# A fixed instruction order from a search, paced loads and 64x64 turns at the start of an attention and FFN kernel

## The chip, the cores and the metric

The kernel runs on one core of a Trainium2 chip. The metric is the device time of one execution in microseconds. A profile shows one execution: its span is the time from the first to the last instruction, and its engines are PE (TensorE's matmuls), PEld (TensorE's weight loads), DVE (VectorE), ACT (ScalarE), POOL (GpSimd) and SP (SyncE, which only issues DMAs).

## What is computed

Attention with squared relu instead of softmax, and a gated FFN on the result:

```python
# q, k, v: (8, 12, 448, 64) float32
scores = q @ k.T / sqrt(64)
attn = maximum(scores, 0) ** 2 / 448
x = (attn @ v)              # -> 3584 tokens x 768
out = (maximum(x @ w_gate, 0) * (x @ w_val)) @ w_out     # 768 -> 1536 -> 768, float32
```

## The kernel before

**Tiling.** Four heads of one batch row make a quad; there are 8 x 3 quads. A quad's keys lie on partitions 64 to 127 and its queries on 0 to 63, in seven slots of 64 positions (`NT`). For its scores the quad has to be turned, so that the head dimension lies on the partitions: for batch row 0 by `transpose_first` (L540 and L547 hold the transposes), for row 1 by `transpose_pe` (L588), for the rest by a DMA transpose on SP (`transpose_dma`, L618, after a permuting copy L610 or L612). L513 and L515 copy the turned quad out of PSUM. A score step (`Attention.s`, L686) multiplies 64x64 tiles, four array positions at a time; relu (L697 on ScalarE, L699 on VectorE) and square (L709, L711) follow, then the product with the values (`pv`, L728) and its copy to `xT` (L744, L746). Row 0 is done in two parts, 192 and 256 positions of its queries, so that the FFN can begin early.

**FFN.** `gv_plain` (L793) is the gate and value product of rows 0 and 1, in blocks of 128 columns of the weights. Later rows go in pairs by a Strassen scheme (`gv_strassen`, L902; `out_both`, L1017), with evictions of partial products to float32 tiles `f` (L849, L851 on ScalarE; L853, L855 on VectorE) and sums by VectorE (L1007). Outputs leave by `store` (L989): two DMAs on SP per tile, for the last ones one on SP and one on ScalarE.

**Loads.** GpSimd's DMAs (`dma_in`, L404) cast float32 to bf16 on the way; keys, queries and values come per quad, the weights in column blocks (`load_gv`) and quarters (`load_out`). At most eight are out at a time. For quad 0, the queries' first three slots come as float32 by two hardware DMAs (L455, on ScalarE's and SP's queues, 96 KB each) and are cast by VectorE (L457); its keys are the first two DMAs of GpSimd.

**Order.** `plan` is a list scheduler that runs when the program is built. It has a time for each operation, gives an operation to the engine that ends it first, takes PSUM banks and buffers as they come free, and fills TensorE's modelled gaps in the first 32 us with matmuls on a constant tile (`filler`, L1171), which compute nothing. Three strings (`PE_ORDER`, `LOAD_ORDER`, `AHEAD`) set the order on TensorE, that of the loads, and priorities. The instructions are issued in the order of the planned starts; each engine works its own off in that order.

Of the kernel before, what the change touches and what calls it, by code (L numbers as in the profile page):

```python
# [15 lines left out]
class Res:  # L16


    def __init__(self, n):
        self.free = {i: 0.0 for i in range(n)}  # L20
        self.by = {}

    def at(self, i):

        t, op = self.free[i], self.by.get(i)
        return t if op is None else max(t, op.end + Planner.LATE[1])


class Buf:


    def __init__(self, res, among=None, width=1):
        self.res, self.width = res, width
        self.among = among if among is not None else sorted(res.free)
        self.readers, self.last, self.idx = 0, 0.0, None

    def pick(self, now=0.0):

        best = None
        for i in self.among:  # L40
            if all(i + w in self.res.free for w in range(self.width)):
                t = max(self.res.at(i + w) for w in range(self.width))
                if best is None or max(t, now) < max(best[0], now):
                    best = (t, i)
        return best


class Op:


    def __init__(self, engs, emit, deps=(), alloc=(), reads=(), mode=None, grp=None):
        self.engs, self.emit = engs, emit
        self.deps, self.alloc, self.reads = list(deps), list(alloc), list(reads)
        self.mode, self.grp = mode, grp
# [4 lines left out]
        self.start = self.end = self.eng = None  # L59
        for b in self.reads:  # L60
            b.readers += 1


class Planner:
    NOUT = 8
    SWITCH = 0.1
    BIAS = 0.2
    MARGIN = 1.5
    LATE = (2.0, 1.0, 0.3)
    TO_LOAD, LOADED = 2.35, 0.95  # L70
    TO_TURN, TURNED, TURN = 1.7, 0.8, 3.65
    ISSUE = 0.28
    TO_HW = 1.9
    COLD = 4.6, 1.6
    FILL_FROM = 0.4
    FILL_COLD = 5.5
    FILL_UNTIL = 32.0
    FILL_MARGIN = 0.1
    GV_ORDER = '1256734'
    OUT_ORDER = 'ab1cd572364'  # L80
    END_ORDER = ('517364', '523')
    BUFFERS = (3, 11, 3, 4, 4, 4, 3)
    PV_PAIRS = (0, 0)
    JOIN = True
    TWO_QUEUES = True
    SPLIT = False
    MERGE = False
    URGENT = {'sh': -0.5, 'perm': 0.5}
    YIELD = {'sq': 0.1, 'sh': 0.1}
    PV_AT_0 = 0  # L90
    QT = 3
    PART = 6
    PV_AT = (1, 1)
    T_AT = (1, 1)
    MORE_UNTIL = 6
    BY_PE = 6
    ORDER = 'LV610ab2c3x4oy5rzqp'

    def __init__(self, banks):
        self.banks = banks  # L100
        self.t = {"POOL": 1.25, "DVE": 0.85, "ACT": 0.74, "SP": 0.74}
        self.ops = []
        self.mode = None
        self.dma_t = 0.0
        self.queues = [], []
        self.loads = []

    def free_at(self, bank):
        return self.banks.free.get(bank, 1e9)

    def now(self, op):
        return self.t.get("PE", 0.0) if "PE" in op.engs else 0.0

    def ready(self, op):
        r = 0.0
        for d in op.deps:
            if d.end is None:
                return None
            if d.eng != "PE" or "PE" not in op.engs:
                r = max(r, d.end + (self.LATE[0] if d.xbar else self.LATE[2] if d.load else 0.0))  # L120
        for b in op.alloc:
            p = b.pick(self.now(op))
            if p is None:
                return None
            r = max(r, p[0])
        return r

    def best(self, op):
        r = self.ready(op)
        if r is None:  # L130
            return None
        c = None
        for e, (occ, busy) in op.engs.items():
            if e in ("DVE", "ACT"):
                r = max([r] + [d.end + self.MARGIN for d in op.deps if d.load and not d.hw])
            s = max(r, self.t.get(e, 0.0))
            if e == "PE" and op.mode != self.mode:
                s = max(r, self.t.get(e, 0.0) + self.SWITCH)
            f = s + busy + (self.BIAS if e == "DVE" and len(op.engs) > 1 else 0.0)
            if c is None or f < c[0]:  # L140
                c = (f, s, e)
        return c[1], c[2], r

    def rates(self, a, b):

        if not (a and b):
            return 1.0, 1.0
        share = a[0][0].share
        return 1.0 - share, share

    def flow(self, a, b, t, until):
        while t < until and (a or b):
            rates = self.rates(a, b)
            d = min([q[0][1] / r for q, r in zip((a, b), rates) if q] + [until - t])
            t += d
            for q, r, post in zip((a, b), rates, (self.LOADED, self.TURNED)):
                if q:
                    q[0][1] -= d * r
                    if q[0][1] < 1e-6:
                        q.pop(0)[0].end = t + post  # L160
# [1124 lines left out]
```

## Time and profile before

| | us |
|---|---|
| device time, median of 3 runs (401.0 to 403.32) | 402.75 |
| span of the profiled execution | 402.3 |
| TensorE busy | 393.8 |
| VectorE busy | 326.1 |
| ScalarE busy | 274.0 |
| GpSimd busy | 75.7 |
| fillers L1171 on TensorE | 34 matmuls |
| first FFN matmul (L793) starts at | 27.5 |

The profiled execution's span is 0.4 us under the median of the runs. The page gives busy time by engine; its second part cuts the span into 40 slices and writes the busy share of each in tenths, with the granted TensorE clock below. The chain of waits follows the last instruction back to what released it, step by step, and so shows which engine set the end at each moment. Windows give the busy time of every engine in chosen stretches.

### The profile page before, as it was taken

The numbers are of one execution on the slowest core, as the hardware profiler recorded it, in microseconds if no ns is written. First come the engines' busy times: TensorE is split into PE (matmuls) and PEld (weight loads), VectorE is DVE, ScalarE is ACT, GpSimd is POOL, SyncE is SP. The second block draws the span as 40 slices with busy tenths as digits, with TensorE's granted clock in tenths as the row PEclk, the third lists the DMA queues.
The fourth block names the chain that finished last, engine by engine and source line by source line (L and its number), as shares of the span: only waits on it lengthen the run. The fifth ranks groups of instructions, "written<-read, shape, count | busy, mean of one in ns | idle before, by whom it ended". The sixth has DMA issues, their size and how long they took to land.

```text
span 402.3 us, 8737 instructions
## 1 busy us (share of the span) xinstructions
PE 393.8 (98%) x3472; PEld 210.1 (52%) x3472; DVE 326.1 (81%) x568; ACT 274.0 (68%) x399; POOL 75.7 (19%) x121
## 2 busy tenths in 40 slices
PE   6999999999999999999999999999999999999995
PEld 3567745454455554444455554444555555555563
DVE  5688788999989879969988989888789967758662
ACT  3697786477979728969879868878788843333221
POOL 7946441020430110311030221300100000000000
PEclk9799999999999999999999999999999999999999
DMA  8999999948988995193698796682224320000245
GB/s 121 192 198 199 201 193 183 147 48 136 124 144 171 162 116 115 26 145 56 84 141 153 152 131 129 82 92 47 46 37 99 80 59 2 0 0 2 59 118 139
DMA packets 77337, 43.54 MB, mean 108 GB/s; under 512 B 40688, under 2 KB 77296, under 8 KB 77296
## 3 DMA queue, kind: packets, MB, share of 16 engines
q0 software_dynamic: 34640, 23.50, 43.1%
q1 hardware_dynamic: 42192, 18.98, 26.5%
q8 instruction: 27, 0.44, 0.5%
q10 hardware_dynamic: 464, 0.49, 0.4%
q14 instruction: 14, 0.11, 0.1%
HBM read 47.19 MB, written 11.01 MB: 145 GB/s over the span
## 4 chain that ended last, share of the span: by engine, by line
PE 95%; DMA 1%; DVE 1%; POOL 0%; issue 0%; ACT 0%; POOLq 0%
PE ps L902 36%; PE ps L1017 25%; PE ps L793 14%; PE ps L686 10%; PE ps L728 8%; DMA gvT<-in_q_dram 1%; PE ps L1171 1%; PE ps L540 1%; PE ps L588 1%; DVE at L711 1%; POOL gvT L404 0%; DVE at L699 0%; DVE qkT L515 0%; DVE f L853 0%; ACT xT L744 0%
## 5 line engine op out<-in xcount | busy, mean ns | idle before, releaser
L697 ACT ACTIVATE at<-ps 128x896 bf16<-128x896 f32 (+4 forms) x116 | 103.2, 906 | 22.6 <-PE ps L686 21.8
L849 ACT COPY f<-ps 128x448 f32<-128x448 f32 x99 | 52.1, 532 | 45.8 <-PE ps L902 34.2
L709 ACT ACTIVATE at<-at 128x896 bf16<-128x896 bf16 (+1 forms) x72 | 67.0, 947 | 2.0 <-DVE at L699 1.2
L711 DVE TENSOR_TENSOR at<-at 128x896 bf16<-128x896 bf16 (+4 forms) x99 | 58.9, 607 | 9.2 <-ACT at L697 8.1
L699 DVE TENSOR_SCALAR at<-ps 128x896 bf16<-128x896 f32 (+4 forms) x55 | 58.4, 1064 | 6.9 <-PE ps L686 6.2
L404 POOL DMA_DIRECT2D vv<-in_v_dram x44 | 26.7, 611 | 165.5 <-PE ps L686 152.5
L686 PE MATMUL ps<-qkT 64*64 64x448 bf16 (+2 forms) x756 | 51.5, 342 | 1.0 <-ACT xT L744 0.3
L902 PE MATMUL ps<-xT,gvT 128*128 128x448 bf16 x216 | 50.9, 353 | 0.0
L902 PE MATMUL ps<-sx,wv 128*128 128x448 bf16 x216 | 50.6, 353 | 0.1
L902 PE MATMUL ps<-xT,wg 128*128 128x448 bf16 x216 | 49.7, 353 | 0.0
L902 PEld LDWEIGHTS <-gvT 128*128 128x128 bf16 x324 | 30.7, 98 | 30.5 <-issue 3.2
L1017 PEld LDWEIGHTS <-sh 128*128 128x128 bf16 x312 | 29.5, 98 | 22.9 <-issue 3.6
L1017 PEld LDWEIGHTS <-hT 128*128 128x128 bf16 x270 | 25.3, 98 | 20.5 <-issue 4.5
L1017 PE MATMUL ps<-wo,hT 128*128 128x384 bf16 x192 | 35.6, 327 | 0.0
L686 PEld LDWEIGHTS <-qkT 64*64 64x64 bf16 x756 | 19.5, 106 | 27.5 <-issue 22.4
L728 PE MATMUL ps<-at,vv 64*64 64x448 bf16 (+2 forms) x700 | 33.4, 327 | 0.0
L1007 DVE SCALAR_TENSOR_TENSOR o<-ps,f 128x384 f32<-128x384 f32 x41 | 22.5, 554 | 12.1 <-PE ps L1017 7.2
L902 PEld LDWEIGHTS <-wv 128*128 128x128 bf16 x216 | 20.6, 98 | 21.0 <-issue 2.8
L793 PE MATMUL ps<-xT,wv 128*128 128x448 bf16 (+2 forms) x180 | 31.3, 316 | 0.0
L902 PEld LDWEIGHTS <-wg 128*128 128x128 bf16 x216 | 20.6, 98 | 19.9 <-issue 1.7
L851 ACT ACTIVATE f<-ps 128x384 f32<-128x384 f32 x37 | 18.2, 491 | 18.6 <-PE ps L1017 18.3
L793 PE MATMUL ps<-xT,wg 128*128 128x448 bf16 (+2 forms) x180 | 30.6, 315 | 0.0
(72 smaller groups left out, 495.5 us busy)
## 6 DMA issues: line engine op xcount, KB each, us to landing
out_dram<-o SPq DMA_DIRECT2D x108, 96.0 KB, 2.2
vv<-in_v_dram POOLq DMA_DIRECT2D x44, 112.0 KB, 5.1
raw<-in_k_dram POOLq DMA_DIRECT2D x18, 224.0 KB, 5.4
raw<-in_q_dram POOLq DMA_DIRECT2D x18, 224.0 KB, 6.0
wo<-in_moe_w_out_dram POOLq DMA_DIRECT2D x4, 576.0 KB, 16.7
wg<-in_moe_w_gate_dram POOLq DMA_DIRECT2D x5, 384.0 KB, 9.9
wv<-in_moe_w_val_dram POOLq DMA_DIRECT2D x5, 384.0 KB, 10.6
gvT<-in_k_dram POOLq DMA_DIRECT2D x5, 224.0 KB, 6.3
```

What stands on the lines that cost most here:

```text
L404: op = Op({"POOL": (0.5 + 0.0004 * n_desc,) * 2}, lambda: nc.gpsimd.dma_start(out=dst(), in_=src), deps=deps, alloc=alloc)
L686: nc.tensor.matmul(banks()[64 * j:64 * j + 64, z, h2], lhsT=self.k_of(j, h2, k), rhs=self.q_of(j, h2), start=True, stop=True)
L697: nc.scalar.activation(self.at_of(i, m), banks(), AF.Relu)
L699: nc.vector.tensor_scalar_max(self.at_of(i, m), banks(), 0.0)
L709: nc.scalar.activation(a, a, AF.Square)
L711: nc.vector.tensor_tensor(a, a, a, ALU.mult)
L728: nc.tensor.matmul(ps[64 * h2:64 * h2 + 64, ps2.idx + j, :n], lhsT=st.v_of(j, h2, c), rhs=self.at_of(c)[64 * j:64 * j + 64, 0, h2], start= ...
L793: nc.tensor.matmul(ps[:, pb.idx, z * n:(z + 1) * n], lhsT=w[:, kd, fc], rhs=xT_t[xbuf[b].idx][:, kd, cols], start=(kd == 0), stop=(kd == K ...
L849: nc.scalar.copy(dst, src)
L902: nc.tensor.matmul(ps[:, pb.idx, :S], lhsT=w(g)[:, fc], rhs=rhs, start=start and g == 0, stop=stop and g == KH - 1, skip_group_check=True)
L1007: op = Op({"DVE": V384}, lambda: nc.vector.scalar_tensor_tensor(o_t[ob.idx], ps[:, pb.idx, :OH], float(out_scale), f_t[fb.idx][:, :OH], AL ...
L1017: nc.tensor.matmul(ps[:, pb.idx, :OH], lhsT=lhs(kf), rhs=rhs(kf), start=start and kf == 0, stop=kf == FH - 1, skip_group_check=True)
```

## The change

1. The scheduler is gone. `PLAN`, a string of some 5,300 characters, holds the order of all operations and fillers, the engine of each and every buffer and bank; `replay` reads it. The classes keep only what `replay` needs, and options that had one value are written out.
2. `hold_back` runs ahead of each of the first 46 loads of GpSimd. It goes back over the issued loads until their modelled times sum to 4.5 us, and has GpSimd copy one element of the load before these; that copy waits until the load has landed.
3. Quad 0's keys (all) and queries (three slots) come as float32 by the hardware queues of ScalarE and SP, 448 and 192 KB, and are cast in two and one operations. They are kept slot by slot with the heads side by side, so that one transpose turns two heads (`paired`).
4. Turns by TensorE are made of 64x64 transposes; keys and queries go to separate PSUM banks and are copied out whole.
5. A store may be issued from SP or from ScalarE; the plan says which.

The order that results: TensorE has 6946 instructions before and 7126 after. Fillers go from 34 to 24. The transposes on TensorE are 36 of 128x64, 48+48 of 64x64 and 84 of 128x64 before; 20 with 64 rows by 128 columns and 296 of 64x64 after. Changes of the array's shape go from 155 to 138 in all, and from 133 to 130 counted from the first L793 on. All other matmuls are the same in number and shape. GpSimd has 30 of the one-element copies. VectorE has 568 instructions before and 596 after; ScalarE issues 22 stores instead of 4, and 33 evictions (21 of 448 and 12 of 384 columns) go from ScalarE to VectorE.

```diff
-PE_ORDER = (...)
-LOAD_ORDER = (...)
-AHEAD = (...)
+IN_FLIGHT, HELD = 4.5, 46
+PLAN = (...)
+def replay(ops, filler):
+    text = iter(PLAN)
...
+    while True:
...
+        if i == FILL:
+            filler(number(), number(), number(2))
+            continue
+        left.remove(i)
+        op = ops[i]
+        op.eng = list(op.engs)[number() if len(op.engs) > 1 else 0]
+        for b in op.alloc:
+            b.idx = number()
+        op.emit()

+    seen = pool.tile([1, 1], BF16, name="seen")
+    issued, waited = [], [-1]
+    def hold_back():
+        k, held = len(issued), 0.0
+        if k >= HELD:
+            return
+        while k > 0 and held < IN_FLIGHT:
+            k -= 1
+            held += issued[k][1]
+        k -= 1
+        if held >= IN_FLIGHT and k > waited[0]:
+            d = issued[k][0]
+            at = d[tuple(slice(0, 1) for _ in d.shape)].rearrange(FLAT[len(d.shape)])
+            nc.gpsimd.tensor_copy(seen[0:1, 0:1], at)
+            waited[0] = k

     def dma_in(dst, src, n_desc, us, deps=(), alloc=(), share=0.25):
-        op = Op({"POOL": (0.5 + 0.0004 * n_desc,) * 2}, lambda: nc.gpsimd.dma_start(out=dst(), in_=src),
-                deps=deps, alloc=alloc)
+        def emit():
+            d = dst()
+            hold_back()
+            issued.append((d, op.load))
+            nc.gpsimd.dma_start(out=d, in_=src)

     def first_loads(st, src):
-            k_op = dma_in(lambda: st.raw()[64:128, hs], src(k)[:, hs], 128, 0.05)
-            ld = Op({eng: (0.65, 0.65)}, lambda: queue.dma_start(out=wide[0:64, hs], in_=src(q, 0, QT)[:, hs]))
-            cv = Op({"DVE": (0.46, 0.55)}, lambda: nc.vector.tensor_copy(st.raw()[0:64, hs, :QT], wide[0:64, hs]), deps=[ld])
+        kl = fetch(k, slice(64, 128), NT, "ACT", nc.scalar, 3.6)
+        ql = fetch(q, slice(0, 64), QT, "SP", nc.sync, 3.4)
+        st.k_ops = [narrow(kl, slice(64, 128), slice(2 * j, 2 * j + 2), NT, True) for j in range(2)]
+        st.q_ops = [narrow(ql, slice(0, 64), slice(0, 4), QT, True)]

+    def turn(bank_of, st, a, slots, js=(0, 1), shift=0):
+        rows = slice(64 * a, 64 * a + 64)
+        for t in slots:
+            for j in js:
+                pb, c = bank_of(a, j)
+                cols = slice(c + (t - shift) * P2, c + (t - shift + 1) * P2)
+                if st.paired and not shift:
+                    nc.tensor.transpose(ps_b[:, pb.idx, cols], st.paired(rows)[:, t, 2 * j:2 * j + 2].rearrange("p h d -> p (h d)"),
+                                        ident[rows, rows])
+                    continue
+                for h2 in range(2):
+                    x = st.late()[:, 2 * j + h2, t - shift] if st.paired else st.raw()[rows, 2 * j + h2, t, :]
+                    nc.tensor.transpose(ps_b[64 * h2:64 * h2 + 64, pb.idx, cols], x, ident[rows, rows])

     def transpose_pe(b, g):
-                        nc.tensor.transpose(ps_b[64 * h2:64 * h2 + 64, ps2.idx + j, t * 128:(t + 1) * 128],
-                                            st.raw()[:, 2 * j + h2, t, :], ident)
-        op = pe(emit, 0.93, deps=st.qk_ops + [id_op], alloc=[ps2, st.qt_buf], mode="128x64")
+            for t in range(NT):
+                for a in range(2):
+                    turn(lambda a, j: (pbs[a], j * S), st, a, (t,))
+        op = pe(emit, 0.47, deps=st.qk_ops + [id_op], alloc=[*pbs, st.qt_buf], mode="64x64")

     def store(ob, op, where):
-        for eng, queue, zs in (("SP", nc.sync, (0,)), ("ACT", nc.scalar, (1,))) if last else (("SP", nc.sync, (0, 1)),):
+        for engs, zs in ((("SP",), (0,)), (("ACT",), (1,))) if last else ((("SP", "ACT"), (0, 1)),):
```

More of the change, by code (lines that the diff above doesn't have):

```diff
@@ L372 @@
     f_t = [pool.tile([128, S], FP32, name=f"f{i}") for i in range(N_F)]
[L373 removed]
+    g_t = [pool.tile([128, S], BF16, name=f"g{i}") for i in range(N_G)]
     o_t = [pool.tile([128, OH], FP32, name=f"o{i}") for i in range(N_O)]
@@ new lines, in narrow @@
+        def narrow(ld, rows, hs, slots, act):
+            n = (hs.stop - hs.start) * slots * D
+            cv = Op({"DVE": (0.08 + n / 1850.0, 0.15 + n / 1850.0)}, None, deps=[ld])
+            if act:
+                cv.engs["ACT"] = vec(n)["ACT"]
+            cv.emit = lambda: copy_out(cv.eng, paired(rows)[:, :slots, hs], wide[rows, hs, :slots].rearrange("p h t d -> p t h d"))
+            cv.kind = "wide"
+            others.append(cv)
+            return cv
+        kl = fetch(k, slice(64, 128), NT, "ACT", nc.scalar, 3.6)
@@ L1160, with filler @@
     others.extend([still_op, id_op])
[L1162 to L1175 removed]
+    def filler(bank, n, width):
+        for _ in range(n):
+            nc.tensor.matmul(ps[:, bank, :width], lhsT=still[:, :128], rhs=still[:, :width], start=True, stop=True)
     for g in range(NQ):
@@ L1251 @@
         out_both(2 * p, p + 2, To_ops)
-    for op in plan(first, att, ffn, others, pool_ops, still_op, filler, r_ps):
-        op.emit()
+    replay([*sum(first, []), *att, *[o for o, _ in ffn], *others, *pool_ops], filler)
 _INS = ['q', 'k', 'v', 'moe_w_gate', 'moe_w_val', 'moe_w_out']
```

596 lines of the change are left out of this document (209 added, 387 removed).

## The prediction

> **What bounds the kernel now.** I read the page from the top: busy shares and slices first, then windows over the start, the chain of waits, and TensorE's timeline.
>
> ```profile
> PE 393.8 (98%) x3472; PEld 210.1 (52%) x3472; DVE 326.1 (81%) x568; ACT 274.0 (68%) x399; POOL 75.7 (19%) x121
> ...
> PE   6999999999999999999999999999999999999995
> ...
> PEclk9799999999999999999999999999999999999999
> ```
>
> TensorE is busy nearly everywhere; only the first slices and the last are thinner, and only the second has a lower granted clock. "Busy" includes L1171, matmuls on a constant tile that fill modelled gaps and compute nothing. So I ask how much of the start is real work. These windows are cut where the granted clock changes (5.47, 8.88, 15.70) and where the first real FFN matmul starts, L793 at 27.5 us in the timeline; columns are busy us and instructions of each engine, clock, DMA share, GB/s.
>
> ```profile
> 5.47:8.87 3.40, 1.96 (x45) 1.02 (x43) 1.67 (x4) 1.44 (x3) 2.19 (x5) 1.00 1.22 167
> 8.88:15.70 6.82, 6.64 (x87) 3.60 (x87) 3.53 (x8) 3.50 (x5) 5.95 (x9) 0.50 1.38 192
> 15.71:27.50 11.79, 10.58 (x288) 7.32 (x287) 10.15 (x19) 10.43 (x16) 7.83 (x11) 1.00 1.50 194
> ```
>
> From 5.47 to 15.70 VectorE and ScalarE work 10.1 of 20.4 engine-us (1.67+3.53+1.44+3.50): 50%. From 15.71 to 27.50 it is 20.6 of 23.6: 87%. They relu, square and copy the scores that the FFN needs, and in the first stretch they lack scores. The start is bound by the arrival of the first three quads, then by these two engines. Afterwards the chain is TensorE's own:
>
> ```profile
> 9.06 1.53 PE ps L540 x19
> ...
> 39.19 0.91 PE ps L588 x28
> 40.10 0.50 PE ps L686 x8
> ...
> 68.03 0.38 PE ps L686 x8
> 68.41 11.46 PE ps L793 x60
> ...
> 326.01 44.28 PE ps L902 x234
> ...
> 372.81 25.36 PE ps L1017 x156
> ```
>
> 44.28/234 = 0.189 us per 448 columns and 25.36/156 = 0.163 per 384: no room there. Eight score matmuls take 0.38 us behind others of their shape, 0.50 when the array shape has just changed; 60 FFN matmuls take 11.46 instead of 60 x 0.189 = 11.34. **A change of array shape costs about 0.12 us.** TensorE ends at 398.2; the last add, its two stores and the closing waits take the other 4.1 us.
>
> **The change, part by part.** The sum is against this execution's span, 402.3 us, 0.4 under the median 402.75 of the runs; I add the difference to the median.
>
> *FFN and later, from the first L793 on.* The matmuls are the same ones. (a) Three quads are turned by 56 transposes of 64x64 each instead of 28 of 128x64 (L588, 0.91 a quad). The 64x64 form exists in L547, two positions at a time:
>
> ```profile
> 16.96 0.69 PE L547 MATMUL ps<-ident,gvT 64*64 64x64 bf16 x32 [0.41 <-DVE at L699]
> ...
> 24.46 0.44 PE L547 MATMUL ps<-ident,gvT 64*64 64x64 bf16 x16
> ```
>
> Sixteen more cost 0.25 us, 15.6 ns each. The new form goes over both halves of the rows and both of the columns, four positions: between 7.8 ns each (0.44 a quad) and 15.6 (0.87). I take 0.50: the scores of L686 use four positions, and eight of them cost two columns' streams (0.38 = 2 x 0.189). 3 x (0.91-0.50) = 1.2 us; bounds 0.1 to 1.4. (b) In the two orders I count changes of shape from the first FFN matmul on: 133 before, 130 after; 3 x 0.12 = 0.4. (c) Twelve more 256-column score matmuls stand ahead of that point: 3 x 0.109 = 0.3. The new order also moves 33 evictions from ScalarE to VectorE (0.62 and 0.55 us each, groups L853 and L855) and 18 store issues from SP to ScalarE (0.5 us each in the trace); fewer relus and narrow copies on VectorE give some back. VectorE goes from 326 to about 342 us, 87% of a 393 us stretch; nothing on it becomes the bound, but its cover is thinner. Sum: 1.9 us.
>
> *The start.* The new TensorE order holds 24 filler matmuls in place of 34. Quad 0's keys and queries come as fp32 by the hardware queues, 640 KB issued at 0.74 us, and are narrowed on VectorE and ScalarE; GpSimd begins with quads 1 and 2. Before, two hardware loads of 96 KB took 3.3 and 3.5 us to land. I estimate 4.0 to 5.0 for the larger ones, so 4.8 to 5.7. Two casts of 896 elements (0.35 us for 384, so about 0.6 each), the turns and the copies put the first scores at 6.9 (6.3 to 8.0), against 6.85: no gain there. The gain is behind it. On GpSimd's queue, 752 KB lie up to the last query that quads 1 and 2 need, 864 before; before, that byte count landed at 10.0 and 10.6 us. All their turns stand together ahead of their scores, so these flow from about 10.3; before, quad 1's began at 10.4 and quad 2's at 13.0, at half clock. Early relus of quad 0 cover 9 to 10.3. I let both engines be dense from 9.0.
>
> Their work up to the first FFN matmul: 30.7 engine-us from 5.47 on (10.1+20.6), plus 2.0 for wider casts and 0.9 for more, smaller copies: 33.6. About 5 are done by 9.0 (casts 2.0, first copies 1.3, first relus and squares). 28.6 at 87% (the third window) need 16.4 us, at 93% (VectorE 4.78 and ScalarE 4.52 in 25 to 30 us) 15.4. The first FFN matmul comes at **24.9** (23.9 to 26): 2.6 us earlier.
>
> The clock belongs to it. It was 1.00 for 3.4 us with TensorE busy 1.96 of them, then 0.50 for 6.8. The new order has ten fillers and the turns just there, so I expect it to stay at 1.00. [...]
>
> *Loads.* Weights come behind. In the old order the tightest weight landed 3.7 us before its use (34.2, used 37.9). Reading the new GpSimd order by bytes against the old issues and landings of the trace, with the FFN at 24.9: one key load at 31.0 against a turn at 30.4; weights at 36.0, 37.9 and 42.1 against 36.4, 38.1 and 42.0. The slack is gone: 0.5 us lost. *Holding back* adds 30 one-element copies on GpSimd, each waiting for a landing, with the next DMA issue behind it. No copy of GpSimd is in the trace: between a 0.035 us step (its four memsets) and a whole square of VectorE, 0.61 (L711). I take 0.2: 30 x 0.2 = 6 us, beside 30 us of issues in the first 46 us, hidden while the queue keeps the 4.5 us of transfers that the code's constant allows. At the upper end it is the second rival.
>
> Sum: 2.6+1.9-0.5 = 4.0 faster: 398.3 in span, **398.7 us**; own range 396.5 to 400.5.
>
> **Rivals.** *Loads become the bound* (0.17). For it: slack 0 to 0.7 us at four places between 30 and 45 us. Against: the DMA is full anyway (about 195 GB/s until 60 us). Loads 5% slower are 1.8 us late at 42: 400.5.
>
> *GpSimd starves the loads, slower than before* (0.10). Each copy reads SBUF while VectorE runs squares back to back. If each waits a whole one, 30 x 0.61 = 18.3 on top of 30 us of issues make 48 in 46 us: the queue runs dry between issues, and loads are 4 to 6 us late by 45 us with nothing to cover it. With 6.5 lost: 405. It decides from about 0.5 us a copy. [...]
>
> *The start gains little* (0.15): hardware loads land late (the change not doing what it says), or the clock drops again and eight fillers take 2.8 us instead of 1.4. FFN from 26.7: 400.5.
>
> *The fixed order stalls* (0.08): engine, bank and order are written out, and the old chain shows one such wait of TensorE (0.64 us on an eviction of VectorE's, L853 at 239.4). Four more of 0.6 us each: 401.
>
> **Chances.** Forecast 0.50. About 0.5% (2 us) is what a measurement of this kernel tells from no change, so faster is below 400.7 and slower above 404.8. Forecast 0.50, plus 0.10, 0.08 and 0.02 of the first, third and fourth rival: faster 0.70; same 0.19; slower 0.11 (second rival 0.10, strays 0.01). The range leaves out the second rival and some 0.08 at the ends: 396.5 to 402.5.
>
> **What would show it.** Right: first FFN matmul near 25 us; granted clock 1.00 from about 5.5 us on; VectorE and ScalarE over 85% busy from 10 us; turns of 0.5 us; waits of TensorE for DMA under 1 us in 28 to 45; TensorE's end near 394. Wrong: a clock of 0.50 past 9 us, turns near 0.9, waits for wg or wv, GpSimd copies over 0.5 us, or an FFN start beyond 26.5.

## The result and the profile after

The changed kernel takes **419.07 us** (median of 4 runs, 417.86 to 419.98) beside 403.03 for the kernel before (4 runs, 401.0 to 404.13): ratio 1.0408, 95% interval 1.0363 to 1.0454. It is 16 us slower; the forecast was 398.7, and its range ended at 402.5. The profiled execution has a span of 417.0 us. Medians here and below are of all runs of a kernel; ratios leave out a single slow run, over 1.5% above the fastest of its kernel, which six of the kernels below have.

The page after, its busy shares, its slices and the granted clock:

```profile
PE 395.5 (95%) x3562; PEld 209.0 (50%) x3562; DVE 333.4 (80%) x596; ACT 259.6 (62%) x374; POOL 81.3 (19%) x149
...
PE   7798989989997999999999899999999999999996
...
PEclk9999999999997999999999899999999999999999
```

A slice is 10.4 us. TensorE's now have dips at 31 to 42, 52 to 63, 83 to 94, 125 to 136 and 229 to 240 us, and the granted clock is below full in two slices, the 13th (125 to 136 us) and the 23rd (229 to 240). To place the loss I line the two traces up by work: at which time has each done the same share of the useful matmuls? The changed kernel is 2.1 us ahead at 24 us, just before its first FFN matmul (26.1), level at 36, 0.8 to 1.3 ahead at 42 to 55, 1.4 behind at 72, 3.3 at 91, 4.6 at 124, **10.4 at 141, 15.3 at 253**, and keeps that to the end. So the last 160 us are alike, and the loss is made in a slow slope up to 124 us and in two steps.

TensorE's waits in the changed kernel, longest in total first (us in total, times, longest):

```profile
PE ps L901 <- DVE o L891: 5.4, 2, 3.0
PE ps L569 <- DVE xT L628: 1.7, 1, 1.7
...
PE ps L610 <- DMA gvT<-in_v_dram: 1.4, 1, 1.4
...
PE ps L569 <- issue: 1.1, 1, 1.1
...
PE ps L675 <- DMA wg<-in_moe_w_gate_dram: 0.7, 1, 0.7
```

The two waits of the first line are the two steps. Four timelines of the changed kernel around the first (start, length, engine, line, operation; in brackets the idle time before it and what ended it): TensorE, VectorE, SP's queue, GpSimd's queue.

```profile
130.83 2.08 PE L901 MATMUL ps<-wo,hT 128*128 128x384 bf16 x6 [3.00 <-DVE o L891]
```
```profile
124.78 0.55 DVE L891 SCALAR_TENSOR_TENSOR o<-ps,f 128x384 f32<-128x384 f32 x1
125.25 0.62 DVE L509 COPY perm<-raw 128x1792 bf16<-128x1792 bf16 x1
130.22 0.56 DVE L891 SCALAR_TENSOR_TENSOR o<-ps,f 128x384 f32<-128x384 f32 x1 [4.35 <-DMA out_dram<-o]
```
```profile
118.43 2.90 SPq L515 DMA_TRANSPOSE qkT<-perm  x2
121.39 3.72 SPq L871 DMA_DIRECT2D out_dram<-o  x4
125.93 4.56 SPq L515 DMA_TRANSPOSE qkT<-perm  x2
```
```profile
122.32 1.20 POOL L263 DMA_DIRECT2D vv<-in_v_dram  x2 [8.49 <-PE ps L610]
123.49 0.65 POOL L263 DMA_DIRECT2D raw<-in_k_dram  x1
124.10 0.64 POOL L263 DMA_DIRECT2D vv<-in_v_dram  x1
124.69 0.68 POOL L263 DMA_DIRECT2D raw<-in_q_dram  x1
126.16 0.61 POOL L263 DMA_DIRECT2D raw<-in_k_dram  x1 [0.79 <-DVE perm L509]
```

An output tile is written at 116.5 us; its store stands on SP behind two DMA transposes and leaves at 121.4. Then GpSimd sends six loads within 5 us. The store issued at 123.67 lands at 130.09, 6.4 us later; the constant in the code (`st.land`) is 2.5. VectorE needs that tile, waits 4.35 us with everything behind it, and TensorE, whose PSUM bank it should empty, waits 3.0. VectorE's waits for output tiles, summed over the trace:

```profile
DVE o L891 <- DMA out_dram<-o: 8.0, 3, 4.4
```

What that does to the clock shows in windows (busy us, instructions, of PE, PEld, DVE, ACT, POOL; clock; DMA; GB/s):

```profile
126.36:129.76 3.40, 1.47 (x14) 0.60 (x7) 0.00 (x0) 1.75 (x2) 0.41 (x1) 1.00 1.15 179
129.77:136.60 6.83, 5.77 (x24) 2.24 (x24) 5.95 (x11) 2.46 (x4) 0.00 (x0) 0.50 1.32 158
...
228.76:232.16 3.40, 1.02 (x10) 0.63 (x7) 1.47 (x4) 3.37 (x5) 0.00 (x0) 1.00 1.47 220
232.17:235.58 3.41, 3.41 (x13) 1.57 (x12) 2.33 (x5) 0.51 (x2) 0.00 (x0) 0.50 0.69 159
```

Each wait brings TensorE to half clock, for 6.83 and 3.41 us; the first drop begins 1.1 us before its wait has ended. Wait and half clock together are the steps of 5.8 and 4.7 us, taken between the same points of the work in both traces. 6.83 is twice 3.41, and the windows of 3.40 us ahead of the two drops have TensorE busy 1.47 and 1.02 us.

The traces say more on it. In each of the 20 profiled executions the drops begin on a grid of 3.41 us (in the changed kernel at 129.77, 232.17 and 416.49 us, 30 and 54 steps apart; in the kernel before at 8.88 and 401.41, 115 steps; the last one of each lies behind TensorE's end), and the grid lies elsewhere in each execution. Cut along it, all 14 windows at full clock with TensorE busy under 0.45 of the window were followed by half clock. Between 0.45 and 0.6 some were and some were not: 1.96 of 3.40 us (0.58) was, at the start of the kernel before, while the window of 88.81 to 92.22 us of the changed kernel, busy 0.51, was not, and a wait of 3.1 us in the run with the copies in the old order (below) fell on two windows, busy 0.59 and 0.51, and was not. So what a wait costs depends on where it falls on the grid as well as on its length.

In the kernel before, stores issued between 120 and 140 us land as slowly (median 5.5 us, longest 7.8), yet in the profiled execution VectorE never waits for a tile: its order has slack there. In a second look at that kernel (below) VectorE waits once, 1.6 us at 123.9, and TensorE not at all.

### The profile page after: what moved, and what is told of

Same layout as the page of the kernel before. It is cut to its first block, busy times and chain, and to the rows that moved or that the text cites. A ratio compares the mean times of both kernels' runs of the same rounds, so it can differ in the third digit from the quotient of the medians.

```text
span 417.0 us, 8952 instructions
## 1 busy us (share of the span) xinstructions
PE 395.5 (95%) x3562; PEld 209.0 (50%) x3562; DVE 333.4 (80%) x596; ACT 259.6 (62%) x374; POOL 81.3 (19%) x149
## 4 chain that ended last, share of the span: by engine, by line
PE 73%; DMA 19%; POOL 3%; issue 2%; SPq 1%; DVE 1%; ACT 0%; POOLq 0%; DVEq 0%
PE ps L784 35%; PE ps L901 23%; PE ps L569 6%; DMA wg<-in_moe_w_gate_dram 6%; PE ps L610 5%; PE ps L675 4%; DMA wo<-in_moe_w_out_dram 4%; DMA wv<-in_moe_w_val_dram 3%; DMA out_dram<-o 3%; DMA gvT<-in_k_dram 3%; POOL seen L252 1%; SPq L871 1%; POOL gvT L263 1%; POOL raw L263 0%; DVE o L891 0%
## 5 line engine op out<-in xcount | busy, mean ns | idle before, releaser
L579 ACT ACTIVATE at<-ps 128x896 bf16<-128x896 f32 (+4 forms) x121 | 105.8, 902 | 37.2 <-PE ps L569 36.5
L731 ACT COPY f<-ps 128x448 f32<-128x448 f32 x78 | 41.0, 537 | 54.3 <-PE ps L784 26.0
L591 ACT ACTIVATE at<-at 128x896 bf16<-128x896 bf16 (+2 forms) x73 | 67.3, 949 | 4.1 <-DVE at L581 3.6
L581 DVE TENSOR_SCALAR at<-ps 128x896 bf16<-128x896 f32 (+2 forms) x50 | 54.0, 1089 | 18.0 <-PE ps L569 17.5
L593 DVE TENSOR_TENSOR at<-at 128x896 bf16<-128x896 bf16 (+4 forms) x98 | 57.2, 607 | 4.1 <-ACT at L579 3.8
L569 PE MATMUL ps<-qkT 64*64 64x448 bf16 (+2 forms) x756 | 52.9, 342 | 5.0 <-DVE xT L628 1.7
L675 PE MATMUL ps<-xT,wg 128*128 128x448 bf16 (+2 forms) x180 | 31.2, 315 | 1.1 <-DMA wg<-in_moe_w_gate_dram 0.7
L263 POOL DMA_DIRECT2D raw<-in_k_dram x18 | 11.4, 631 | 104.4 <-DVE perm L509 93.1
L901 PE MATMUL ps<-wo,sh 128*128 128x384 bf16 x156 | 31.5, 342 | 0.0
## 6 DMA issues: line engine op xcount, KB each, us to landing
wo<-in_moe_w_out_dram POOLq DMA_DIRECT2D x4, 576.0 KB, 10.1
```

The costliest lines, as they stand in the source:

```text
L263: nc.gpsimd.dma_start(out=d, in_=src)
L569: nc.tensor.matmul(banks()[64 * j:64 * j + 64, z, h2], lhsT=self.k_of(j, h2, k), rhs=self.q_of(j, h2), start=True, stop=True)
L579: nc.scalar.activation(self.at_of(i, m), banks(), AF.Relu)
L581: nc.vector.tensor_scalar_max(self.at_of(i, m), banks(), 0.0)
L591: nc.scalar.activation(a, a, AF.Square)
L593: nc.vector.tensor_tensor(a, a, a, ALU.mult)
```

## The experiments

Theory A: the written-out order needs output tiles back too soon for stores that share the DMA with loads. B: holding back starves the early loads. C: the one-element copies themselves cost. D, formed on the way: TensorE's instructions arrive late.

### Stores beside loads (A)

**Late loads left out.** `dma_in` issues nothing for q, k, v of rows 4 to 7.

```diff
-            nc.gpsimd.dma_start(out=d, in_=src)
+            if not left_out:                       # left_out = b >= 4
+                nc.gpsimd.dma_start(out=d, in_=src)
```

> The changed kernel without GpSimd's loads of q, k and v for batch rows 4 to 7 (issued from 106 us on); these rows are computed from what lies in the buffers. Theory A with the loads as the cause of the slow stores (five to seven loads are issued within 4 us just ahead of the stores, and both kinds of packets alternate on the same DMA engines): the stores land in 2.5 to 3 us, the waits of TensorE for o at 131 and 231 us and the half clocks behind them go: 407 to 410. If the DMA transposes on SP's queue are the cause instead: both waits stay, 416 to 419. Theory B: all of its loss lies earlier, 416 to 419 too unless the waits go.

Measured: 409.49 us, ratio to before 1.0173 (1.0112 to 1.0234). Stores of 120 to 140 us land in 2.23 us (median; 4.08 in the changed kernel). Of the two waits this is left:

```profile
PE ps L903 <- DVE o L893: 1.1, 2, 0.7
```

That is within 407 to 410: the loads are the main cause of the slow stores. In the changed kernel, from 123.7 to 130.1 us, 1147 packets of GpSimd's queue and SP's begin, and from one to the next the queue changes 373 times.

**Transposes left out.** `for a in range(2 if b < 4 else 0)` around the DMA transpose.

> The changed kernel without the DMA transposes of batch rows 4 to 7 on SP's queue (the copies ahead of them stay; scores of these rows use what lies in the buffers). Theory A with the loads as the cause: the stores still land 5 us or more after their issue in both places, at least one of the two waits of TensorE stays, 411 to 418. Theory A with the transposes as the cause (stores queue behind them on SP, and share the DMA): both waits go, 407 to 410.

Measured: 414.32 us, 1.0291 (1.0221 to 1.0361). Both waits stay (4.5 us in total, longest 2.4), the first step shrinks by 2.9 us. That is within 411 to 418, for the loads as the cause; the transposes have a part in it, the smaller one.

**Stores on ScalarE's queue.** `if op.land and len(op.engs) > 1: op.eng = "ACT"` in `replay`.

> The changed kernel with all stores but the last ones issued by ScalarE; SP keeps the DMA transposes. At the first place the store of a tile written at 116.5 us is issued at 121.4 us, behind two DMA transposes on SP, and then meets the loads. Theory A with SP's queue as half of the cause: that store leaves at 117, the wait of TensorE at 131 us goes or falls under 1 us; the second place (stores ahead of the transposes, behind the loads) stays: 411 to 415. If only the loads count: both waits stay, 417 to 420. ScalarE is 62% busy and has 0.5 us more per store issue; if that costs, 420 to 424.

Measured: 427.28 us, 1.0565 (1.0491 to 1.064), worse than all that was expected. ScalarE now waits itself for an output tile (4.45 us at 135.5), TensorE 3.7 us for it, and more of the same comes at 404 and 413 us.

```profile
ACT o L735 <- DMA out_dram<-o: 12.0, 3, 5.3
...
PE ps L571 <- ACT o L735: 3.7, 1, 3.7
```

A free queue is no remedy where the engine behind it has other work.

**Late loads paced.** Here nothing is left out: `hold_back` goes on after the 46th load with 1.2 in place of 4.5 us of transfers in flight; in the second kernel it goes on only from the 56th load.

```diff
-        if k >= HELD:
+        if HELD <= k < FROM:                       # first kernel: FROM = HELD = 46; second: FROM = 55
             return
-        while k > 0 and held < IN_FLIGHT:
+        most = IN_FLIGHT if k < HELD else LATER    # LATER = 1.2
+        while k > 0 and held < most:
```

> The changed kernel with the holding back carried on for the loads after the 46th, at 1.2 us of modelled transfers (about one load of a quad at a time). Theory A with the loads as the cause: fewer packets of loads stand beside the stores, which land in 3 to 4 us, the waits for o shrink to under 1.5 us each, 409 to 414, if the loads themselves don't come too late. If they do (each load then waits for the one before it, some 2.5 us apiece, 10 us per quad against about 14 us between quads): new waits of TensorE for q, k, v, 418 to 425. Rival: no change, 418 to 420.

Measured: 420.98 us, 1.0385 (1.0293 to 1.0476). Both effects are there: the steps shrink by 5.0 and 2.2 us, but w_out, now held too, lands late, VectorE waits 9.8 us for it and TensorE 8.5:

```profile
DVE woT L720 <- DMA wo<-in_moe_w_out_dram: 9.8, 1, 9.8
...
PE ps L568 <- DVE xT L627: 8.5, 1, 8.5
```

> The changed kernel with the holding back carried on at 1.2 us of modelled transfers from the 56th load on (from 85 us; the loads of w_out and of rows 2 and 3 ahead of it go out as they are). Carried on from the 47th load, it cut the two waits for o tiles by 5.0 and 2.1 us but made w_out 9 us late. Theory A with the loads as the cause: the gain stays and that loss goes, 411 to 414. Rival (the two effects hang together): 418 to 421.

Measured: **408.78 us**, 1.014 (1.008 to 1.0199): 10 us better than the changed kernel, with the same work. GpSimd's queue at the first place (line numbers are higher by one):

```profile
123.83 0.18 POOL L253 COPY seen<-vv 1x1 bf16<-1x1 bf16 x1 [2.84 <-DMA vv<-in_v_dram]
124.28 0.62 POOL L264 DMA_DIRECT2D raw<-in_k_dram  x1 [0.28 <-issue]
124.89 0.18 POOL L253 COPY seen<-vv 1x1 bf16<-1x1 bf16 x1
125.02 0.60 POOL L264 DMA_DIRECT2D vv<-in_v_dram  x1
125.66 0.32 POOL L253 COPY seen<-vv 1x1 bf16<-1x1 bf16 x1
125.92 0.62 POOL L264 DMA_DIRECT2D raw<-in_q_dram  x1
130.71 0.29 POOL L253 COPY seen<-raw 1x1 bf16<-1x1 bf16 x1 [4.17 <-DMA raw<-in_k_dram]
```

The loads come two or three at a time, with copies between them, some of which wait (2.84 and 4.17 us here). The stores of 121.0 and 122.7 us land in 3.8 and 2.6 us, and VectorE's waits for tiles are 1.7, 0.7 and 0.5 us:

```profile
DVE o L892 <- DMA out_dram<-o: 3.0, 3, 1.7
```

Theory A holds: two experiments, one that leaves loads out and one that spreads them, take the same 10 us away. In the traces 8 us of it lie at the two steps, which shrink from 5.8 and 4.7 us to 1.3 and 1.1 with the loads left out, and to 0.9 and 1.5 with the loads paced.

**Output tiles in turn.** The plan names tile 2 for the eviction at 130.2 us; another tile had been free since 126.3. The old order took its four tiles in turn at that stage, the plan does not. Here `replay` takes the tile whose last store was issued longest ago, in the changed kernel and in the one with paced late loads.

```diff
             b.idx = number()
+            if b.res.free is not None:             # output tiles alone
+                b.idx = b.res.free.pop(0)
         op.emit()
+        for b in op.reads:
+            b.readers -= 1
+            if b.readers == 0 and b.res.free is not None:
+                b.res.free.append(b.idx)
```

> The changed kernel with the output tile of each eviction chosen in the order in which tiles come free in the program (the one whose last store was issued longest ago) in place of the plan's number; order, engines and queues as in the plan. At the first place the plan names the tile whose stores land at 130.1 us, while the stores of another had landed at 126.3. Theory A in this sharper form (the plan reuses tiles out of turn, since its model has them free): VectorE's wait of 4.35 us there falls to under 1 and the half clock goes, the second place (the tile there is the oldest one already) keeps its 2.4 us: 411 to 415. Theory A in the plain form (four tiles are too few for such stores): the waits move and stay, 417 to 420.

> The same choice of tiles together with late loads paced from the 56th on at 1.2 us (408.8 alone). If pacing has taken both steps already: 407 to 410. If the remaining waits for tiles (1.7, 0.7 and 0.5 us) go with it: 405 to 407. Below 403, better than the kernel before, only if the slope of the first 91 us went too, which nothing here touches.

Measured: 413.96 us, 1.026 (1.021 to 1.0311), and 408.63, 1.0107 (1.0058 to 1.0155). The total of the first is as the sharper form had it, the places are not. VectorE's wait of 4.35 us falls to 0.7 and 0.5, but the wait moves: ScalarE stands 4.2 us for a tile at 133.5, and TensorE 3.0 us for ScalarE.

```profile
PE ps L580 <- ACT o L744: 3.0, 1, 3.0
```

The first step shrinks by less than 1 us, the second by 2.7. The rest of the 5 us came ahead of both, before the first output tile is written (116 us), where this edit does nothing; 1.5 us of it is an earlier start. With paced loads the choice of tiles adds nothing that can be told. So the plain form holds at the first place: four tiles are too few for stores that land so late, whichever is taken.

### Holding back the early loads (B, C)

**Without the copies** (`HELD = 0`).

> The changed kernel without the 30 one-element copies on GpSimd (HELD = 0); all else as it is. Theory A (output tiles: in two places the stores of o tiles take 6 to 7 us to land, VectorE waits for a free tile, TensorE waits 3.0 and 2.4 us and runs at half clock for 6.8 and 3.4 us; about 10 of the 16 us): both places lie long after the last copy (62 us), so both waits stay, and only the early part gains: 414 to 418. Theory B (holding back starves the loads: weights 2 us late at 36 to 40, 10 us late at 64, w_out and raw late at 90; that is 4 to 5 us by 124 us and shifts all that follows against the loads): with the copies gone the loads land as before, the early lag goes, 412 to 415, and if the lag brought the two later waits about, 402 to 405. Theory C (the copies themselves slow VectorE or GpSimd): as B for the early part, but the loads' landings stay.

Measured: 419.19 us, 1.0383 (1.0321 to 1.0445): no change, and outside what each of the three theories had for it. What landed at 36 to 46 us comes 2 us earlier, what landed at 56 to 64 comes 8 to 11 earlier, but something new takes it back (windows of this kernel, columns as above):

```profile
31.24:33.96 2.72, 0.00 (x0) 0.00 (x0) 0.00 (x0) 1.24 (x2) 2.03 (x3) 0.86 1.41 200
33.96:40.00 6.04, 6.04 (x85) 4.13 (x85) 4.22 (x6) 2.17 (x4) 2.62 (x4) 0.50 1.49 195
```

TensorE stands still for 2.7 us at 31.2 and then runs at half clock for 6 us. The trace names no releaser for that wait ("issue"); the section on fetching finds it.

**The copies alone in the old order.** `hold_back` and its call in `dma_in`, put into the kernel before.

> The kernel before with the holding back of the changed one alone (one-element copies ahead of GpSimd's first 46 loads, by the same constant of 4.5 us). Theory B: fewer loads are out beside the DMA transposes between 45 and 65 us, the loads come late there, TensorE waits for weights, 3 to 6 us slower: 406 to 409. Theory A: the old order has slack for it, no new wait for o tiles, 402.5 to 404.5. Theory C: as B, but with the loads' landings as before.

Measured: 408.3 us, 1.0107 (1.004 to 1.0174). Loads 42 to 46 land 6 to 8 us later than in the kernel before, and TensorE waits for them:

```profile
PE ps L758 <- DMA gvT<-in_v_dram: 3.1, 1, 3.1
...
PE ps L758 <- DMA vv<-in_v_dram: 1.3, 1, 1.3
```

B is right for the old order, as far as this edit goes. C is wrong: in the changed kernel a copy takes 0.18 us.

```profile
L252 POOL COPY seen<-gvT x11: 176/177/676, 7.2 to 58.6; 1x1 bf16<-1x1 bf16 x11
```

(ns: shortest, median, longest.) Ten of the 30 copies take longer, 0.20 to 0.68 us: each of these ran beside a square of VectorE (L593) and ended 0.04 us behind the end of one. The other 20 took 0.18; 12 of them began beside other work of VectorE (L398, L581, L628, L685), and one 0.13 us ahead of a square. The mean is 0.26. What costs is the waiting. GpSimd's copy at 58.6 us had waited 7.2 us for values issued at 45.6 and landed at 58.45, and no load was issued meanwhile. Windows over 40 to 55 us, the changed kernel and then the one before:

```profile
40.00:55.00 15.00, 14.86 (x206) 10.62 (x205) 11.72 (x21) 12.60 (x19) 7.47 (x15) 1.00 1.50 146
```
```profile
40.00:55.00 15.00, 15.00 (x180) 9.60 (x177) 11.50 (x20) 11.97 (x18) 7.96 (x12) 1.00 1.37 199
```

146 GB/s in place of 199, though the DMA engines' share is higher.

**Holding ended at the 34th load**, with the late pacing (`HELD, FROM, LATER = 34, 55, 1.2`).

> The changed kernel with late loads paced as before, and the early holding back ended at the 34th load (issued at 41 us) instead of the 46th. Theory B in this form (between 41 and 62 us the queue stands nearly empty beside the DMA transposes, and v, wg and w_out come 8 to 10 us late): the waits at 58, 64 and 90 us (1.4, 0.7 and 1.7 us) go, 404.5 to 406.5. Rival (with more loads out, instruction fetches or transposes come later and give it back, as when all copies were left out): 408 to 411.

Measured: 409.28 us (404.6 to 415.86, 6 runs), 1.0106 (1.0044 to 1.0168): not to be told from 408.78. In its trace TensorE's waits at 58 and 64 us (v, wg) are gone, the one at 90 us (w_out) stays, 1.5 us. The time is the one of the rival, 408 to 411; that it has the rival's reason is not shown.

**Rows 2 and 3 left out.** Meant to leave out rows 2 to 7; as built, the condition let the loads of rows 4 to 7 through. So row 2 is replaced by memsets, row 3 by nothing, and the rest is loaded.

> The changed kernel without GpSimd's loads of q, k and v for batch rows 2 to 7: those of row 2 are replaced by GpSimd memsets of the same tiles, those of rows 3 to 7 by nothing, so these rows are computed from constants and old data; weights and rows 0 and 1 are loaded as before. Theory A widened (the written-out order is tight around loads and stores that land later than its model, early and late; the order itself is as good as forecast): weights land early, the waits for v, wg, w_out and o go, and the time comes near the forecast, 398 to 402. Rival (the order, the turns or the start are worse in themselves, whatever the transfers do): 404 to 409, as with rows 4 to 7 left out.

> The kernel before with the same loads left out (row 2 by memsets, rows 3 to 7 by nothing). Theory A widened: the old order already hides its loads and stores, so nothing is gained, 401.5 to 403.5. Rival (any order gains by idle DMA engines, by faster SBUF or an earlier start): 395 to 400, and the changed kernel's gain from the same edit is then no proof against its order.

Measured: the changed kernel 410.1 us, 1.016 (1.01 to 1.0219); the kernel before 402.04, 0.9989 (0.9952 to 1.0026). The old order hides these loads; the new one does not. The changed kernel misses its 398 to 402. The loads of rows 4 to 7, still there, have a part in that: the two later steps remain (4 and 3 us). From the FFN's begin to 91 us the changed kernel loses 5.4 us against before, and 2.3 with rows 2 and 3 left out. But each figure belongs to one execution. In the six others that have the changed kernel's work up to 85 us (late loads or late transposes left out, stores on ScalarE, late pacing, tiles in turn, the last two together) the loss is 2.2 to 4.3, more where the FFN began earlier, and in three of them the waits for v and wg at 58 and 64 us are missing. In the next experiment, also without rows 2 and 3, it is 0.9. So these loads have a part in the slope, and its size is not shown.

**All of rows 2 to 7 left out**, by the mended condition.

> The changed kernel without GpSimd's loads of q, k and v for rows 2 to 7, all of them this time: row 2's replaced by memsets, rows 3 to 7's by nothing (the runs before took out rows 2 and 3, and rows 4 to 7). Theory A widened: late loads of weights, v and w_out cost 4 to 6 us up to 91 us, and stores beside loads some 10 us behind it; both go, 398 to 402, next to the forecast. Theory D alone: the fetch waits stay (1.6 us), 402 to 404. Rival (the order stalls in itself): 406 to 410.

Measured: 404.09 us, 1.0004 (0.997 to 1.0037). The slope (0.9 us) and both steps are as good as gone, and the new order is level with the old one; the forecast's gain is not there even then. That is 2 us above the range of theory A (398 to 402) and just above D's (402 to 404); a fetch wait of 1.5 us remains.

### Instruction fetch (D)

All waits of TensorE of 0.3 us or more that the trace puts down to "issue", in all profiled executions of the new order, lie at the same numbers when TensorE's instructions (matmuls, weight loads and its few semaphore instructions) are counted from 0 in the trace: 449, 705, 961 or 1217, steps of 256. There is none in the four of the old order with its fillers uncut (the kernel before twice, with the copies, and without rows 2 and 3); the longest there is 0.28 us, at 705 too. The DMA view of the changed kernel lists packets of a kind of their own:

```profile
q8 instruction: 28, 0.46, 0.5%
```

28 packets of 16 KB for some 7140 instructions: 256 each. Counted from the moment at which a block of 256 is entered:

```
kernel              block   entered   16 KB packet      next block entered   wait
before              449     18.2 us   +3.6 .. +4.6      +6.0                 0.28
before              705     24.2      +3.8 .. +4.7      +6.3                 -
before              961     30.6      +3.6 .. +4.5      +7.1                 -
changed             449     16.5      +3.1 .. +3.9      +5.6                 0.53
changed             961     28.5      +2.2 .. +3.4      +4.6                 1.07
changed, no copies  961     27.6      +3.9 .. +4.9      +6.3                 2.72
```

The last column is the wait at the next block's entry. Wherever TensorE waited there, the next block was entered 1.2 to 1.7 us after its packet had landed, and nowhere sooner. Up to 35 us, while loads fill the DMA (183 to 199 GB/s from 5 to 30 us in the changed kernel), the packet has landed 1.2 to 5.0 us after the block before was entered. From number 449 to 1217 the old order takes 5.4 to 7.2 us for 256 instructions, over its four executions; the new one, its wait taken off, mostly 3.5 to 5, and waits. Such a wait was up to 2.7 us long, with a half clock behind it.

**Old turns in the new order** (`TALL = (3, 4, 5)`, a constant of the code), with and without the copies.

> The changed kernel with row 1's three quads turned by 28 transposes of 128x64 each, as in the kernel before, in place of 56 of 64x64 (the copies behind them fit to it). Theory D (instruction fetch): in every run of the new order TensorE's unexplained waits stand at its instructions number 449, 705, 961 or 1217, steps of 256; a DMA packet of 16 KB of kind instruction lands 1.2 to 1.5 us before each ends. A turn of 56 transposes holds 112 instructions, one of 28 holds 56, so the denser stream runs dry. Then the wait at number 1217 (1.1 us in the changed kernel, 2.7 without the hold copies) falls under 0.5, while each turn takes 0.9 us again (0.51, 0.65 and 0.80 now): 416 to 420 in all. Rival (that wait is for the turned quad's load or a PSUM bank): it stays at 1 us or more at the same work.

> The same turns of 128x64 in the changed kernel without the 30 hold copies. Without the copies alone, the loads landed 2 us earlier at 36 to 46 us and 9 us earlier at 54 to 64, but a wait of 2.7 us at instruction 1217 and a half clock behind it took 4.6 us and the total stayed at 419. Theory D: with fewer instructions that wait and the half clock go, and the early landings show in the time, 412 to 416. Rival: wait and half clock stay, 418 to 421.

Measured: 414.84 us, 1.0259 (1.0194 to 1.0324), and 415.95, 1.0303 (1.0236 to 1.037). The first is below D's 416 to 420, the second within its 412 to 416, with the half clock at 34 to 40 us gone. D's forecast of the wait's size failed: it does not fall under 0.5 but is 1.21 and 1.28 us. It is still at number 1217, which is now other work (the end of a turn and not its beginning, 56 instructions further on). That this wait kept the number and not the place speaks for the fetch, and against data or a bank. The 4 us that the first gains lie at 58 and 90 us, where waits for v and xT are missing, and partly in an earlier start; why is not settled.

**Late pacing and old turns together.**

> The changed kernel with late loads paced (from the 56th on, at 1.2 us) and row 1 turned by 128x64 transposes. Alone, the first took 419 to 408.8, the second to 414.8. If they add up: 403 to 406; if the second's gain was only a shift of the waits for o tiles, which the pacing has taken already: 407 to 410.

Measured: 408.83 us (406.0 to 412.57, 6 runs), 1.0107 (1.0047 to 1.0167), within 407 to 410: the gains don't add up.

**Denser fillers in the old order.** 34 filler matmuls cut into pieces of 64 columns.

```diff
             for _ in range(n):
-                nc.tensor.matmul(ps[:, pb.idx, :width], lhsT=still[:, :128], rhs=still[:, :width], start=True, stop=True)
+                for c in range(0, width, 64):
+                    w = min(64, width - c)
+                    nc.tensor.matmul(ps[:, pb.idx, :w], lhsT=still[:, :128], rhs=still[:, :w], start=True, stop=True)
```

> The kernel before with its fillers cut into pieces of 64 columns: 188 more matmuls on the constant tile and as many weight loads, nothing else. Theory D: TensorE's instructions come in blocks of 256, a fetch begins 2 to 7 us after a block is entered while loads fill the DMA, so a denser stream runs dry: unexplained waits of 0.3 us or more appear at numbers 193 + 256 k before 30 us, where the old order has none; first FFN matmul 0.5 to 3 us later, 403.5 to 407. Rival (those waits of the new order are for data or banks): no wait at such a number, 402 to 404.

Measured: 410.06 us, 1.0122 (1.0053 to 1.0192). The waits are there, at numbers 961 and 1217:

```profile
PE ps L1173 <- issue: 2.2, 1, 2.2
...
PE ps L728 <- issue: 1.2, 1, 1.2
```

The first FFN matmul comes at 32.0 us and the time lies above 403.5 to 407, both more than expected; how much of that is the pieces' own time is not separated. That a denser stream makes such waits is shown.

### The start

**The kernel before, looked at again**, nothing changed.

> The kernel before, unchanged, looked at again. If the half clock of its start (8.9 to 15.7 us) belongs to the order, it is there again, with the first FFN matmul near 27.5 us. If it is a matter of the single execution (the old start stood at full clock in two runs with edits far behind it, with first FFN matmuls at 26.0 and 25.3 us), it may be gone: 25 to 26 us. Time 400 to 405 either way.

Measured: 402.29 us in one run, span 400.5, the first FFN matmul at **24.8 us** in place of 27.5. Its windows:

```profile
5.47:8.87 3.40, 2.42 (x61) 1.48 (x61) 2.29 (x5) 2.25 (x4) 3.06 (x6) 1.00 1.16 160
8.88:15.70 6.82, 5.53 (x139) 3.40 (x139) 5.49 (x14) 5.36 (x8) 5.27 (x9) 1.00 1.39 194
```

Full clock, and VectorE and ScalarE busy 15.4 of 20.4 engine-us where the first execution had 10.1. Of the four profiled executions with the old order of TensorE's start (this one, the first, and the runs with the copies and without rows 2 and 3) three ran it at full clock, with the first FFN matmul at 24.8, 26.0 and 25.3 us. In those with the new start it came at 24.6 to 28.7. What differs between two executions is not the clock alone, so the 2.7 us between 27.5 and 24.8 are not all shown to be its price.

Do transposes count as busy for the clock? Along the grid of 3.41 us, five windows have TensorE busy under 0.45 without its transposes and yet full clock behind them; the plainest, at 7.9 us of the kernel before without rows 2 and 3, is busy 0.25 without them and 0.72 with them. That speaks against transposes being idle time for it. One window of the kernel before speaks the other way: from 8.88 to 12.29 us, at half clock, TensorE is busy 0.95 with its transposes and 0.42 without, and half clock went on. So it is not settled.

## Why the prediction was wrong

**The steps that failed.** (1) "Nothing on it becomes the bound, but its cover is thinner": I counted VectorE's work (342 us, measured 333) and not what it waits for. Waits for output tiles were priced at nothing; they cost 10 us, two waits of 3.0 and 2.4 us and the half clocks that came with them. That stores moved to another queue was priced at their issue alone; that the move is the cause is not shown. The fourth rival had the mechanism (engine, bank and order are written out), but four waits of 0.6 us: it took its price from an eviction and left out the DMA and the clock. The view that could have told was on hand: stores of the old kernel land in 5.5 us at 120 to 140, with 2.5 in the code that plans them. (2) The start's 2.6 us. The clock stayed at 1.00 as forecast. But the first scores came at 8.5 and not at 6.9 (6.3 to 8.0), both engines were dense from 15 us (10.0 and 10.4 of 10.4 us up to the FFN) and not from 9, and the FFN began at 26.1 and not at 24.9 (23.9 to 26). And the 27.5 that I set against it belonged to one execution with half clock; the old order reaches 24.8. There was nothing to gain, which is the third rival in its effect, though in the profiled execution the clock did not drop and the FFN came before that rival's 26.7. (3) Loads, "0.5 us lost": from the FFN's begin to 91 us TensorE waits 3.8 us for v (1.4), one wg (0.7) and work behind w_out (1.7), and 1.1 for a fetch, which the sum does not have. The slope there is 5.4 us in this execution and 2.2 to 4.3 in others, so its size is known only roughly. The slack was read from landings of the old order, with up to eight loads out; the held queue moves 146 GB/s beside the transposes, not 199.

**What held.** The price of a copy, 0.2 us (measured 0.18 as the median; all 30 took 7.8 us, for 6); the larger hardware load at 4.8 to 5.7 us (5.4; the smaller landed at 6.2, outside); a clock of 1.00 through the start of the profiled execution, though others of the same start show less (0.66 to 0.88 in 5 to 20 us where the late loads were left out). Turns got shorter, 0.51, 0.65 and 0.80 us against 0.90: 0.75 us in all, of 1.2 forecast, and they make the instruction stream denser. The 0.4 for shape changes and 0.3 for scores moved ahead can't be seen beside the rest.

**The rivals.** Neither of the two on loads was the cause as put: the copies are cheap (0.26 us in the mean, where the second rival needed about 0.5), and the waits for late loads are some 4 us of 16. Undoing the holding alone changes nothing: loads land earlier, but in its trace a fetch wait of 2.7 us and a half clock take that back.

**Open.** Why DMA transposes and few loads together move less than with many loads out; why the old turns gain 4 us in the new order; what part of the denser fillers' loss is their own time. Two obvious remedies were not tried: more than four output tiles, and the 33 evictions back on ScalarE. No kernel that leaves nothing out beats the one before; the best of them with the new order are those with paced late loads, 1.1 to 1.4% slower.

## What to carry to other kernels

An order written out from a model is as good as the model's worst constant: compare each one (a store's landing, a load's) with the trace in the stage where it matters, beside the transfers that run there, and look what the engine behind it would then wait for. A wait of TensorE of two or three microseconds can count twice, because half clock may follow it (it did after 3.0 and 2.4 us in the changed kernel, not after 3.1 us in the old order with the copies). Before a gain at the start is counted, look at a second execution of the old kernel.

## What was not expected of the hardware

- TensorE's instructions came by DMA in blocks of 256 (28 packets of 16 KB in the changed kernel), and while loads filled the DMA the next block's packet had landed 1.2 to 5.0 us after a block was entered, and where TensorE waited the block was entered 1.2 us later at the soonest. The old order, with 5.4 to 7.2 us per block from number 449 to 1217, waited 0.3 us for a block nowhere; the new one, with mostly 3.5 to 5, did. A turn of 64x64 pieces holds 112 instructions for 0.51 to 0.80 us of work.
- Stores of 96 KB landed in 2.1 to 2.3 us when little else ran, in 2.7 to 4.2 us in a group of six stores with the late loads left out, and in 2.7 to 9.3 beside five or six loads.
- The clock at the start differs between executions of one kernel: 0.50 or 1.00 in 8.9 to 15.7 us, with the first FFN matmul at 27.5 us in the one execution of the old start with half clock, and at 24.8 to 26.0 in the three without.
- A short wait of TensorE was followed by half clock or not according to how it fell on a grid of 3.41 us: under 0.45 busy in a window always (14 of 14), between 0.45 and 0.6 at times.
